# A three-stage transformer block on one core: last two products of the paired second layers swapped, two groups of additions made by accumulating transfers, places freed sooner, token products halved, and another order

## The chip, the core and the metric

The kernel runs on one core of a Trainium2 chip. The metric is device time in microseconds. Three runs of the kernel before took 1363.52, 1364.46 and 1368.9 us; the median is 1364.46 us. TensorE (PE in the profile) multiplies 128x128 weights, loaded beforehand (PEld), with a moving operand; VectorE (DVE) and ScalarE (ACT) do elementwise work; GpSimd (POOL) adds a little and issues accumulating transfers; SyncE (SP) issues nearly all other transfers.

## The reference

Soft-capped attention, then two residual stages: an MLP behind a layer norm, and a token-and-channel mixer.

```python
batch, n_heads, seq, head_dim = (4, 12, 448, 64)          # d_model 768
scores = cap * np.tanh(scale * (q @ k.T) / cap)
attn = softmax(scores)                                     # max subtracted, 1e-9 in the sum
x = (attn @ v) in (batch, seq, 768)
xn = (x - mean) / sqrt(var + 1e-6) * g_ln
x = x + relu(xn @ w_ch1) @ w_ch2                           # 768 -> 3072 -> 768
u = x + (relu(x.T @ w_tok1) @ w_tok2).T                    # tokens: 448 -> 256 -> 448
out = u + relu(u @ u_w_ch1) @ u_w_ch2                      # 768 -> 1536 -> 768
```

## The kernel before

Activations lie transposed: `X[b]` holds, for one of four batches, six tiles of 128 channels by 448 tokens. Products run with a number split into a rounded high part and a remainder (`split`, `low`, line 176), in three passes (`PASSES`, line 620), so a product over 128 channels is three matmuls of 448 columns. A layer's hidden units are worked in groups of 512: six groups in the first MLP, three in the second stage's channel MLP.

The program has three parts. (1) Attention of batches 0 and 1, then their layer norm. (2) Groups of the MLPs of batches 0 and 1 (`mlp`, `second_layer`), between which the heads of batches 2 and 3 and the token mixing of 0 and 1 (`tokens`) are laid. (3) Batches 2 and 3. Here most groups run as *pairs* (`strassen`, line 869): with seven block products in place of eight, each block product over sums of weight blocks and of the two batches. There are five such pair groups, then token mixing of 2 and 3, then two more. A pair group is one *block* in this text: `first_quads` (line 718) makes its hidden values H1, H2, H3, H4, H11, H21, H22, and `second_quads` (line 784) multiplies them by the second layer's tiles a11, a12, s1, s2, s3, s4, a22, three products of six matmuls for each tile pair.

The tiles a11, a12 and a22 come from DRAM as they are (`direct`). The tiles s1 to s4 are weight sums. `sums` (line 666) makes them by a chain on two working tiles: a plain transfer in (`start`), accumulating transfers issued by POOL (`more`, line 676), a negation on ACT (line 682), a split by ACT or DVE (lines 180, 182, 176) into the tile that PE reads. The working tiles are called `v`, `late_pair`, `late_vs` and `late_qk` in the profile; `late_vs` and `late_qk` serve the second half of a block's columns. The tiles that PE reads are eight half tiles taken in a ring (`part_ring`, line 664): a sum can only be split into a half tile whose last reader is done.

What a second-layer product is worth is added to X on DVE: `plus` (line 701) adds a bank of results, `both` (line 640) adds a finished tile: the lines 849 to 851 add w, the sum of s1 and s2 products, to X[3][r] and X[3][3+r], and line 858 adds t to X[2][3+r]. A block thus has nine such additions to X of one operand that is not a bank. Then come the products by s4 (`plus` into X[3][r]) and by a22 (`plus` into X[2][3+r]).

The order on each engine is made while the program is built. `Program.add` takes each step with the engines it may use, its cost in columns and a due time (`prog.key`); `emit` then hands out steps engine by engine, the earliest due among those that are ready by the planner's own costs (`FIXED`, `RATE`, `LATER`, lines 94 to 97). Engines work through their lists in that order. The numbers in lines 60 to 71 are due times and leads.

Storage is reused: `relay` (line 245) gives places of part 2 new names for part 3. `fill_weights` (line 274) waits for the readers of all old tiles in one list (line 291), `two`, which layer norm 3 uses, among them.

Of the kernel before, what the change touches and what calls it, by code (L numbers as in the profile page):

```python
# [59 lines left out]
URGENT, SCORES, PREPARE, LOAD = 1000.0, 19.31, 4.58, 24.58  # L60
# [4 lines left out]
T_LN0, T_LN1 = 7.69, -20.0  # L65
T_AHEAD, N_AHEAD, AHEAD_PACE = 14.0, 1, 5.0
T_ALONE, STRETCH0, T_PAIR, STRETCH1 = 85.0, 1.3, 165.0, 1.14
T_ATT2, PACE2, T_ATT3, PACE3 = 230.0, 35.0, 650.0, 25.0
LEAD, RAW_AHEAD, EVACUATE, TOKENS_AHEAD = 6.3, 9.57, -7.49, 17.25
N_WARM = 9  # L70
QUAD_LEAD, SUM_LEAD, SIDES_LATER, SIDES_PACE, X_LATER = 16.0, 24.0, 20.0, 4.0, 4.0
# [17 lines left out]
class Program:  # L89
# [5 lines left out]
    RATE = {"place": 0.0, "pe": 202.6e-3 / S, "act": 0.833e-3, "dve": 1.042e-3, "pool": 2.4e-3, "dma": 2.4e-3}  # L95
    LATER = {"pe": 0.16, "act": 0.1, "dve": 0.085, "pool": 0.05, "dma": 3.6}
# [59 lines left out]
def block_kernel(ctx: ExitStack, tc: tile.TileContext, qkv, cap, gln, w1, w2, wt1, wt2, con, out):  # L156
# [88 lines left out]
    def relay():  # L245
# [28 lines left out]
        def fill_weights():  # L274
# [6 lines left out]
            EXTRA[0].at, EXTRA[1].at = t[:, :, :CC], t[:, :, CC:]  # L281
            TWO.at = place("late_two", [2, S], F32R, tag="two")
# [8 lines left out]
        later([*WHOLE, PAIR, *V, *two, *QK, *KS, *VS], [*WF, *EXTRA, TWO, *TMP[:2]], fill_weights)  # L291
# [346 lines left out]

    def both(to, a, b, op, cols, early=0.0):
        add("dve+", cols, lambda: dve.tensor_tensor(to.at, a.at, b.at, op=op), [a, b], [to], early=early)  # L640
# [25 lines left out]
    def sums(chunks, a11, a12, a21, a22, s1, s2, s3, s4):  # L666
# [33 lines left out]
    def plus(to, bank, t):  # L700
        add("dve", S, lambda: dve.tensor_tensor(to.at, bank.at[:, :S], t.at, op=ALU.add), [bank, t], [to])  # L701
# [82 lines left out]
    def second_quads(g, last):  # L784
# [3 lines left out]
        tiles = dict(zip(("a11", "a12", "s1", "s2", "s3", "s4", "a22"), pairs))  # L788
# [50 lines left out]
        further(QUAD_LEAD)  # L839
# [4 lines left out]
        prog.key -= QUAD_LEAD  # L844
        direct("a22", 1, 2 * P)
        prog.key += QUAD_LEAD
        for r in range(3):
# [94 lines left out]
    def tokens(b, hidden):  # L942
# [55 lines left out]
        def second(half, hT):  # L998
            for e in range(3 * half, 3 * half + 3):
# [135 lines left out]
```

## Time and profile before

| | |
|---|---|
| median of three runs | 1364.46 us |
| the profiled execution | 1362.73 us, its span 1361.0 us |
| busy in the span | PE 1317.1, DVE 1160.7, ACT 766.7, POOL 236.6 us |
| parts in the span | heads and norm of batches 0, 1: to about 187; part 2: to about 790; first five blocks: about 838 to 1118; tokens of 2, 3: to 1224; last two blocks: to the end |

The busy time is the union of an engine's instructions. Matmuls overlap, so that what stands as idle before a matmul is somewhat less than what the next one starts late. The stretches of the profile tell where PE waits; the list of waits tells for whom.

### The profile page before, as it was taken

What the parts mean: (1) busy time and instruction counts of PE and PEld (TensorE: products, weight loads), DVE (VectorE), ACT (ScalarE), POOL (GpSimd) and SP (SyncE); (2) the same over time, 40 slices, a digit from 0 to 9 for tenths busy, and PEclk for the clock granted to TensorE, in tenths of its full rate; (3) what the DMA queues carried; (4) which work ended last, traced back from release to release, by engine and by line L of the source; (5) the groups of instructions that cost most, each with busy time, mean ns of one, the idle gap of its engine ahead of it and who ended that gap; (6) DMA issues with size and microseconds to landing.
All of it is one profiled execution on the core that took longest, in us unless ns stands there. A gap on an engine that the chain in (4) does not pass through costs nothing. (4 is left out here: it accounts for less than half of the span.)

```text
span 1361.0 us, 18258 instructions
## 1 busy us (share of the span) xinstructions
PE 1317.1 (97%) x6234; PEld 1128.5 (83%) x6234; DVE 1160.7 (85%) x1999; ACT 766.7 (56%) x1227; POOL 236.6 (17%) x196
## 2 busy tenths in 40 slices
PE   8899999999999999999999999899999999999997
PEld 4334589999999899988899989788988889999786
DVE  5989799999999999999999874878888884476698
ACT  8996667675766756866765322634535442223442
POOL 2420000110101001200000030333323320011221
PEclk9999999999999999999999999999999999999899
DMA  7885357777777868466777587687787884357685
GB/s 279 307 276 194 119 185 250 276 256 284 247 253 263 281 236 279 151 222 224 246 249 246 199 258 246 133 189 168 172 188 166 199 212 143 116 170 184 133 196 129
DMA packets 163021, 290.12 MB, mean 213 GB/s; under 512 B 12016, under 2 KB 105840, under 8 KB 162928
## 3 DMA queue, kind: packets, MB, share of 16 engines
q1 hardware_dynamic: 131888, 266.64, 57.9%
q0 software_dynamic: 30464, 22.03, 11.9%
q8 instruction: 49, 0.80, 0.3%
q10 hardware_dynamic: 576, 0.29, 0.1%
q14 instruction: 44, 0.36, 0.1%
HBM read 203.39 MB, written 85.52 MB: 212 GB/s over the span
## 5 line engine op out<-in xcount | busy, mean ns | idle before, releaser
L899 PE MATMUL bank<-h,split 128*128 128x448 f32 x1452 | 312.4, 368 | 4.0 <-DMA split<-kept 1.8
L926 PE MATMUL bank<-big,split 128*128 128x448 f32 x1404 | 299.2, 368 | 0.5 <-DVE split L176 0.5
L899 PEld LDWEIGHTS bank<-h,split 128*128 128x128 f32 x1452 | 271.4, 188 | 29.2 <-issue 3.6
L926 PEld LDWEIGHTS bank<-big,split 128*128 128x128 f32 x1404 | 262.6, 188 | 25.2 <-issue 1.6
L176 POOL TENSOR_TENSOR ks<-qk,ks 64x512 fp32r<-64x512 f32 x24 | 34.6, 1444 | 497.1 <-ACT ks L419 488.3
L903 DVE TENSOR_TENSOR x<-x,bank 128x448 f32<-128x448 f32 x121 | 73.8, 610 | 24.3 <-PE bank L899 23.6
L180 ACT ACTIVATE split<-whole 128x512 fp32r<-128x512 f32 (+1 forms) x70 | 50.4, 721 | 60.5 <-PE bank L899 24.5
L931 ACT ACTIVATE h<-bank 128x448 fp32r<-128x448 f32 x78 | 42.1, 540 | 64.5 <-PE bank L926 64.3
L333 ACT ACTIVATE whole<-raw 128x512 f32<-128x512 f32 (+2 forms) x94 | 70.7, 752 | 12.5 <-DMA raw<-in_w 6.8
L336 DVE SCALAR_TENSOR_TENSOR whole<-raw,whole 128x512 int32<-128x512 int32 (+2 forms) x94 | 74.1, 788 | 0.1
L337 DVE CUSTOM_DVE_ANT_0 whole<-raw,whole 128x1024 uint16<-128x1024 uint16 (+2 forms) x84 | 71.3, 849 | 0.1
L334 ACT ACTIVATE raw<-raw 128x512 int32<-128x512 uint32 (+2 forms) x94 | 71.2, 758 | 0.1
L176 DVE TENSOR_TENSOR split<-whole,split 128x512 fp32r<-128x512 f32 (+1 forms) x80 | 64.9, 812 | 0.8 <-ACT split L180 0.6
L446 DVE TRANSPOSE_TENSOR_REDUCE m<-x 128x28 f32<-128x896 f32 x48 | 52.9, 1105 | 12.3 <-ACT x L442 11.9
L441 ACT ACTIVATE own<-sc,tsc 128x896 f32<-128x896 f32 x48 | 48.2, 1004 | 15.2 <-DVE x L502 7.9
L713 PE MATMUL bank<-big,split 128*128 128x448 f32 x222 | 52.7, 375 | 2.3 <-ACT split L180 2.2
L932 DVE SCALAR_TENSOR_TENSOR h<-bank,h 128x448 fp32r<-128x448 f32 x78 | 47.7, 611 | 8.1 <-ACT h L931 7.9
L335 DVE TENSOR_SCALAR whole<-whole 128x512 int32<-128x512 int32 (+2 forms) x94 | 52.3, 557 | 1.9 <-ACT whole L333 1.8
L446 DVE TRANSPOSE_TENSOR_REDUCE m<-own 128x28 f32<-128x896 f32 x48 | 52.7, 1097 | 0.9 <-ACT own L442 0.9
L493 DVE TRANSPOSE_TENSOR_REDUCE n<-own 128x28 f32<-128x896 f32 x48 | 52.5, 1097 | 0.0
L442 ACT ACTIVATE own<-own,cap_t 128x896 f32<-128x896 f32 x48 | 50.0, 1042 | 0.6
L438 PE MATMUL sc<-qs,ks 128*128 128x448 f32 x192 | 48.1, 371 | 1.9 <-ACT own L441 1.4
(426 smaller groups left out, 2803.1 us busy)
## 6 DMA issues: line engine op xcount, KB each, us to landing
split<-kept SPq DMA_DIRECT2D x94, 384.0 KB, 4.4
raw<-in_w SPq DMA_DIRECT2D x36, 768.0 KB, 5.4
kept<-split SPq DMA_DIRECT2D x36, 768.0 KB, 4.2
raw<-in_w SPq DMA_DIRECT2D x54, 512.0 KB, 3.8
split<-kept SPq DMA_DIRECT2D x42, 512.0 KB, 3.9
keeps<-split SPq DMA_DIRECT2D x42, 512.0 KB, 3.8
qk<-in_qkv SPq DMA_DIRECT2D x33, 480.0 KB, 4.3
whole<-whole SPq DMA_DIRECT2D x28, 384.0 KB, 2.8
```

The source lines that it names most:

```text
L176: eng.tensor_tensor(out, whole, high.bitcast(F32), op=ALU.subtract)
L333: add("act", m * 1.1, lambda: act(f.bitcast(F32), hi.bitcast(F32), AF.Copy, scale=2.0 ** -112), [r], [w])
L334: add("act", m * 1.1, lambda: act(lo, lo.bitcast(U32), AF.Copy, scale=2.0 ** -29), (), [r])
L335: add("dve+", m // 2, lambda: dve.tensor_scalar(f, f, 3, None, op0=ALU.logical_shift_left), (), [w])
L336: add("dve+", m, lambda: dve.scalar_tensor_tensor(f, hi, -(1 << 31), f, op0=ALU.bitwise_and, op1=ALU.bitwise_or), [r], [w])
L337: add("pool+" if ahead else "dve+", m, lambda e: engine_of[e].tensor_tensor(f, f, lo, op=ALU.add), [r], [w])
L446: add("dve", 2 * S, lambda half=half, e=e: dve.tensor_reduce(m.at[:, half].rearrange("p c j -> p (c j)"), e.rearrange("p c (j i) -> p (c j ...
L493: add("dve", 2 * S, lambda half=half, e=e: dve.tensor_reduce(n.at[:, half].rearrange("p c j -> p (c j)"), e.rearrange("p c (j i) -> p (c j ...
L713: mm(bank.at[:, :S], w(wi), x.at[:, xi], start=(i, n) == (0, 0), stop=(i, n) == (len(parts) - 1, 2))
L899: mm(py.at[:, :S], w[:, wi, i * P:(i + 1) * P], h[i].at[:, hi], start=(i, n) == (0, 0), stop=(i, n) == (G - 1, 2))
L903: add("dve", S, lambda x=x, py=py: dve.tensor_tensor(x.at, x.at, py.at[:, :S], op=ALU.add), [py], [x], early=EVACUATE)
L926: mm(ph.at[:, :S], w[:, wi, cc * P:(cc + 1) * P], src[cc].at[:, xi], start=(cc, n) == (0, 0), stop=(cc, n) == (NCC - 1, 2))
```

## The change

1. `second_quads`: the products by a22 now stand ahead of those by s4; a22 gets the sixth pair of half tiles, s4 the seventh; the step of the chain that splits s4 is due later.
2. `onto`: of the nine additions, six (X[3][3+r] += w and X[2][3+r] += t) become accumulating transfers issued by POOL.
3. `relay`: `late_two` gets a filling of its own, so the rest no longer waits for `two`.
4. `second` in `tokens`: one step of six matmuls becomes two of three, the three of j=0 for each of three banks first.
5. Numbers: due times, leads, and the planner's costs, hence the order on all engines; `plus` has a lead of its own (`FIRST`).

```diff
-URGENT, SCORES, PREPARE, LOAD = 1000.0, 19.31, 4.58, 24.58
+URGENT, SCORES, PREPARE, LOAD = 1000.0, 12.03348, 11.42015, 28.4373
...
-        later([*WHOLE, PAIR, *V, *two, *QK, *KS, *VS], [*WF, *EXTRA, TWO, *TMP[:2]], fill_weights)
+        later([*WHOLE, PAIR, *V, *QK, *KS, *VS], [*WF, *EXTRA, *TMP[:2]], fill_weights)
+        later(two, [TWO], fill_two)
...
+    def onto(to, a):
+        add("pool", CC - 50, lambda: nc.gpsimd.dma_start(out=to.at, in_=a.at, accum_op=ALU.add), [a], [to], early=-X_LATER, lag=3.5)
...
-            add("pool", CC, lambda: nc.gpsimd.dma_start(out=shaped(f, at), in_=at, accum_op=ALU.add), boxes, [f], lag=4.0)
+            add("pool", CC - 50 if len(at.shape) == 2 else CC + 96, lambda: nc.gpsimd.dma_start(out=shaped(f, at), in_=at, accum_op=ALU.add), boxes, [f], lag=3.5)
...
-        tiles = dict(zip(("a11", "a12", "s1", "s2", "s3", "s4", "a22"), pairs))
+        tiles = dict(zip(("a11", "a12", "s1", "s2", "s3", "a22", "s4"), pairs))
...
             both(X[3][r], X[3][r], w[r], ALU.add, S, -X_LATER)
-            both(X[3][3 + r], X[3][3 + r], w[r], ALU.add, S, -X_LATER)
+            onto(X[3][3 + r], w[r])
...
-            both(X[2][3 + r], X[2][3 + r], t[r], ALU.add, S, -X_LATER)
+            onto(X[2][3 + r], t[r])
+            yield
+        for r in range(3):
+            plus(X[2][3 + r], times("a22", r, H4), X[2][3 + r])
+            final(2, 3 + r)
             yield
         for r in range(3):
             plus(X[3][r], times("s4", r, H22), X[3][r])
             final(3, r)
-            yield
-        for r in range(3):
-            plus(X[2][3 + r], times("a22", r, H4), X[2][3 + r])
-            final(2, 3 + r)
             yield
...
+            banks = {}
+            for j in range(2):
+                for e in range(3 * half, 3 * half + 3):
...
-                pe(6 * S, product, [*hT, *T2], [pu])
+                    pe(3 * S, product, [hT[j], T2[j]], [pu])
```

PE, the end of the third block, before. h_88 and h_89 are H3 (products by s3), h_82 and h_83 are H22 (by s4), eh and el are H4 (by a22).

```order
L713 MATMUL bank_111<-h_88,late_whole 128x448 x3
L713 MATMUL bank_111<-h_89,late_whole 128x448 x3
L713 MATMUL bank_112<-h_82,split_73 128x448 x3
L713 MATMUL bank_112<-h_83,split_73 128x448 x3
L713 MATMUL late_bank_5495<-h_82,split_73 128x448 x3
L713 MATMUL late_bank_5495<-h_83,split_73 128x448 x3
L713 MATMUL bank_113<-h_82,split_73 128x448 x3
L713 MATMUL bank_113<-h_83,split_73 128x448 x3
L713 MATMUL late_bank_5496<-eh_100,split_74 128x448 x3
L713 MATMUL late_bank_5496<-el_101,split_74 128x448 x3
```

The same place now:

```order
L719 MATMUL late_bank_5906<-h_88,late_whole 128x448 x3
L719 MATMUL late_bank_5906<-h_89,late_whole 128x448 x3
L719 MATMUL bank_112<-eh_100,split_73 128x448 x3
L719 MATMUL bank_112<-el_101,split_73 128x448 x3
L719 MATMUL late_bank_5907<-eh_100,split_73 128x448 x3
L719 MATMUL late_bank_5907<-el_101,split_73 128x448 x3
L719 MATMUL bank_113<-eh_100,split_73 128x448 x3
L719 MATMUL bank_113<-el_101,split_73 128x448 x3
L719 MATMUL late_bank_5908<-h_82,split_74 128x448 x3
L719 MATMUL late_bank_5908<-h_83,split_74 128x448 x3
```

The eighteen matmuls by a22 stand between s3 and s4.

PE, the first products of part 3, before. A run of nine on `big_80` or `big_81` is a direct product; `late_x`, `late_raw`, `late_own` are the activation sums.

```order
L713 MATMUL late_bank_5495<-late_raw,split_75 128x448 x9
L713 MATMUL bank_112<-late_x_6267,split_74 128x448 x9
L713 MATMUL bank_113<-late_own,split_75 128x448 x6
L713 MATMUL bank_113<-qs_97,split_75 128x448 x3
L713 MATMUL late_bank_5493<-big_80,split_73 128x448 x9
L713 MATMUL bank_111<-big_80,split_73 128x448 x9
```

Now:

```order
L719 MATMUL late_bank_5907<-late_raw,split_75 128x448 x9
L719 MATMUL late_bank_5905<-big_80,split_73 128x448 x9
L719 MATMUL bank_111<-big_80,split_73 128x448 x9
L719 MATMUL bank_112<-late_x_6231,split_74 128x448 x9
L719 MATMUL bank_113<-late_own,split_75 128x448 x6
L719 MATMUL bank_113<-qs_97,split_75 128x448 x3
```

The two direct products of the half tiles `split_73` stand two products (eighteen matmuls) sooner.

DVE, the end of the third block, now. `sq`, `sum`, `other` are w; `rstd`, `late_ks`, `late_qk` are t; L707 is `plus`, L646 is `both`.

```order
L646 TENSOR_TENSOR sq_94<-sq_94,rstd_110 128x448
L707 TENSOR_TENSOR late_ks<-late_bank_5908,late_ks 128x448
L707 TENSOR_TENSOR rstd_110<-late_bank_5905,rstd_110 128x448
L646 TENSOR_TENSOR sum_95<-sum_95,late_ks 128x448
L707 TENSOR_TENSOR late_qk<-bank_114,late_qk 128x448
L646 TENSOR_TENSOR x_79<-x_79,sq_94 128x448
L176 TENSOR_TENSOR split_74<-late_vs,split_74 128x384
L646 TENSOR_TENSOR other_96<-other_96,late_qk 128x448
L707 TENSOR_TENSOR late_ks<-bank_111,late_ks 128x448
L707 TENSOR_TENSOR late_qk<-late_bank_5906,late_qk 128x448
L646 TENSOR_TENSOR x_79<-x_79,sum_95 128x448
L707 TENSOR_TENSOR x_79<-late_bank_5905,x_79 128x448
```

The last row adds s3's first bank to X[3][3]; it now has to wait for the transfer that adds `sq`, which can go out after the first row; ten instructions stand between. Behind it, three rows on, stand the splits of `late_pair` and `v` for the next block. For the six transfers there stand 10, 9, 11, 14, 11 and 12 instructions between.

POOL at the same place, now; L643 is `onto`, L682 is `more`. Before, the L643 rows are not there.

```order
L682 DMA late_pair<-whole_16_180 128x384
L682 DMA late_qk<-whole_17_182 128x384
L643 DMA x_79<-sq_94 128x448
L643 DMA x_79<-sum_95 128x448
L682 DMA v<-whole_18_184 128x384
L643 DMA x_78<-rstd_110 128x448
L643 DMA x_79<-other_96 128x448
L643 DMA x_78<-late_ks 128x448
L643 DMA x_78<-late_qk 128x448
L682 DMA late_vs<-whole_19_186 128x384
```

Six additions stand among the accumulations of the next block's sums.

## Rows read from the trace of the kernel before

**Rows 1.** The page: busy time, share, instructions of each engine

```profile
PE 1317.1 (97%) x6234; PEld 1128.5 (83%) x6234; DVE 1160.7 (85%) x1999; ACT 766.7 (56%) x1227; POOL 236.6 (17%) x196
```

**Rows 2.** Stretches of the span: busy us (instructions), PE clock, DMA share, GB/s

```profile
0.00:102.00 102.00, 91.16 (x299) 38.40 (x300) 80.89 (x126) 92.73 (x119) 32.09 (x25) 0.98 0.82 288
102.00:187.00 85.00, 81.47 (x329) 50.85 (x328) 70.80 (x131) 51.37 (x71) 3.04 (x2) 1.00 0.48 157
187.00:790.00 603.00, 599.55 (x2974) 548.36 (x2973) 581.10 (x966) 396.11 (x602) 62.77 (x44) 1.00 0.70 243
790.00:904.00 114.00, 106.00 (x501) 94.47 (x501) 80.40 (x139) 40.66 (x80) 30.60 (x28) 0.99 0.78 213
904.00:1118.00 214.00, 208.02 (x1006) 187.19 (x1005) 186.95 (x357) 103.75 (x200) 67.71 (x62) 1.00 0.84 185
1118.00:1224.00 106.00, 105.28 (x547) 97.38 (x547) 55.84 (x93) 28.02 (x55) 9.47 (x8) 1.00 0.46 144
1224.00:1361.00 137.00, 125.65 (x587) 111.85 (x585) 104.72 (x194) 54.03 (x104) 30.89 (x27) 0.96 0.67 160
```

**Rows 3.** Timeline of PE at the second layers: start, us, [idle before <-releaser]

```profile
892.37 0.67 PE L713 MATMUL late_bank<-eh,split 128*128 128x448 f32 x2 [1.17 <-DMA split<-keeps]
...
947.53 0.47 PE L713 MATMUL late_bank<-h,split 128*128 128x448 f32 x1 [1.90 <-ACT split L180]
...
1001.16 1.26 PE L713 MATMUL bank<-h,split 128*128 128x448 f32 x3 [1.35 <-ACT split L180]
...
1054.78 1.27 PE L713 MATMUL late_bank<-h,split 128*128 128x448 f32 x3 [0.91 <-ACT split L180]
...
1347.22 1.27 PE L713 MATMUL bank<-h,split 128*128 128x448 f32 x3 [1.04 <-ACT split L180]
```

**Rows 4.** Timeline of ACT: the split of s4's second half, fourth block

```profile
1054.21 0.52 ACT L180 ACTIVATE split<-late_vs 128x384 fp32r<-128x384 f32 x1 [5.60 <-DMA late_vs<-wholes]
```

**Rows 5.** First block: timeline of PE and of ACT

```profile
849.87 2.02 PE L713 MATMUL bank<-big,split 128*128 128x448 f32 x9
...
867.13 2.98 PE L713 MATMUL bank<-big,split 128*128 128x448 f32 x9 [2.22 <-ACT split L180]
...
851.93 0.53 ACT L180 ACTIVATE split<-late_vs 128x384 fp32r<-128x384 f32 x1 [1.31 <-PE bank L713]
```

**Rows 6.** Stretches of 5 us, columns as in rows 2

```profile
865.00:870.00 5.00, 2.74 (x10) 2.26 (x11) 5.00 (x10) 3.82 (x8) 1.28 (x1) 0.89 0.31 63
870.00:875.00 5.00, 5.00 (x21) 4.55 (x20) 3.48 (x7) 3.41 (x8) 1.37 (x2) 0.77 0.57 71
1265.00:1270.00 5.00, 3.26 (x11) 2.62 (x11) 4.30 (x9) 2.69 (x6) 1.28 (x1) 0.83 0.61 131
1280.00:1285.00 5.00, 4.21 (x14) 3.80 (x15) 3.33 (x7) 2.32 (x5) 3.21 (x4) 0.69 0.44 77
```

**Rows 7.** The end: timeline, DVE (first and last of nineteen) and PE's last

```profile
1347.68 0.62 DVE L640 TENSOR_TENSOR x<-x,late_ks 128x448 f32<-128x448 f32 x1
...
1357.28 0.61 DVE L701 TENSOR_TENSOR x<-late_bank,x 128x448 f32<-128x448 f32 x1
...
1353.80 0.77 PE L713 MATMUL late_bank<-el,split 128*128 128x448 f32 x3
```

**Rows 8.** Line 676: duration ns min/median/max, first and last start; landing

```profile
L676 POOL DMA_DIRECT2D v<-whole x21: 859/862/1794, 797.9 to 1301.7; - x21
...
DMA to landing us min/median/max: 3.5/4.7/7.7
```

**Rows 9.** The page: POOL's DMA queue: packets, MB, share of 16 engines

```profile
q0 software_dynamic: 30464, 22.03, 11.9%
```

**Rows 10.** Waits of PE in 1260 to 1285: us in total, times, longest

```profile
PE bank L713 <- DVE late_whole L176: 1.6, 1, 1.6
PE late_bank L713 <- DVE split L182: 1.2, 1, 1.2
```

**Rows 11.** Waits of PE in 170 to 790

```profile
PE bank L1006 <- DVE h L993: 0.9, 2, 0.5
```

More of the change, by code (lines that the diff above doesn't have):

```diff
@@ L94 @@
     FIXED = {"place": 0.0, "pe": 0.0, "act": 0.067, "dve": 0.07, "pool": 0.15, "dma": 0.1}
-    RATE = {"place": 0.0, "pe": 202.6e-3 / S, "act": 0.833e-3, "dve": 1.042e-3, "pool": 2.4e-3, "dma": 2.4e-3}
-    LATER = {"pe": 0.16, "act": 0.1, "dve": 0.085, "pool": 0.05, "dma": 3.6}
+    RATE = {"place": 0.0, "pe": 202.6e-3 / S, "act": 0.833e-3, "dve": 0.001057, "pool": 2.4e-3, "dma": 2.4e-3}
+    LATER = {"pe": 0.16, "act": 0.147286, "dve": 0.047049, "pool": 0.05, "dma": 3.379172}
     ACROSS, ALONG = 0.09, 0.035
@@ L281, in fill_weights, with fill_two @@
             EXTRA[0].at, EXTRA[1].at = t[:, :, :CC], t[:, :, CC:]
+        def fill_two():
             TWO.at = place("late_two", [2, S], F32R, tag="two")
@@ L700, in plus @@
     def plus(to, bank, t):
-        add("dve", S, lambda: dve.tensor_tensor(to.at, bank.at[:, :S], t.at, op=ALU.add), [bank, t], [to])
+        add("dve", S, lambda: dve.tensor_tensor(to.at, bank.at[:, :S], t.at, op=ALU.add), [bank, t], [to], early=FIRST)
     def out_copy(to, bank):
@@ L838, in second_quads @@
             yield
-        further(QUAD_LEAD)
+        prog.key -= QUAD_LEAD
+        direct("a22", 1, 2 * P)
+        prog.key += QUAD_LEAD
         w = [next(tmps) for _ in range(3)]
@@ L843, in second_quads @@
             yield
-        prog.key -= QUAD_LEAD
-        direct("a22", 1, 2 * P)
-        prog.key += QUAD_LEAD
+        further(QUAD_LEAD)
         for r in range(3):
@@ L998, in second, with product @@
         def second(half, hT):
-            for e in range(3 * half, 3 * half + 3):
-                pu, xb, g = next(main_banks), X[b][e], u[e]
-                def product(e=e, pu=pu):
-                    a = (e % 3) * P
-                    for j in range(2):
+            banks = {}
+            for j in range(2):
+                for e in range(3 * half, 3 * half + 3):
+                    if j == 0:
+                        banks[e] = next(main_banks)
+                    pu, xb, g = banks[e], X[b][e], u[e]
+                    def product(e=e, pu=pu, j=j):
+                        a = (e % 3) * P
                         for n, (hi, wi) in enumerate(PASSES):
@@ L1007, in product @@
                                start=(j, n) == (0, 0), stop=(j, n) == (1, 2))
-                pe(6 * S, product, [*hT, *T2], [pu])
-                add("dve", S, lambda xb=xb, pu=pu: dve.tensor_tensor(xb.at, xb.at, pu.at[:, :S], op=ALU.add), [pu], [xb])
-                add("act", S, lambda xb=xb, g=g: act(g.at[:, 0], xb.at, AF.Copy), [xb], [g])
-                add("dve+", S, lambda xb=xb, g=g: low(dve, g.at[:, 1], xb.at, g.at[:, 0]), [xb], [g])
-                yield
+                    pe(3 * S, product, [hT[j], T2[j]], [pu])
+                    if j == 1:
+                        add("dve", S, lambda xb=xb, pu=pu: dve.tensor_tensor(xb.at, xb.at, pu.at[:, :S], op=ALU.add), [pu], [xb])
+                        add("act", S, lambda xb=xb, g=g: act(g.at[:, 0], xb.at, AF.Copy), [xb], [g])
+                        add("dve+", S, lambda xb=xb, g=g: low(dve, g.at[:, 1], xb.at, g.at[:, 0]), [xb], [g])
+                    yield
         hT = yield from first((yield from transposed(0)), False)
```

12 lines of the change are left out of this document (6 added, 6 removed).

## The prediction

> **What bounds the kernel now.** I read the page's busy line first, then the stretches, then PE's waits, and last the timeline around the waits that the change touches. PE is busy for 1317.1 of 1361.0 us [rows 1], and the change adds or removes no matmul. So all that can be won is the time in which PE stands still or runs slowly: 44 us in all. The stretches say where [rows 2]. The first 102 us hold 10.8 us of idle PE, but ACT is busy for 92.7 of them with the heads, so little of it is to be had. From 187 to 790 PE stands for 3.5 us only (603 less 599.55), while DVE is busy 96%. From 790 to 904, the run into the pair groups, it stands for 8.0; in the next four blocks (904 to 1118, 53.5 us each) for 6.0; in the tokens 0.7; from 1224 on for 11.4, of which 6.4 lie behind the last matmul, which ends at 1354.6 [rows 7].
>
> In the blocks the wait that ends last is nearly always one for a weight sum. The second-layer waits [rows 3] are 1.90, 1.35, 0.91 and 1.04 us for the split that makes s4, in the second, third, fourth and last block, and 1.17 for the transfer of a22 in the first. In the fourth block the split itself starts at once when its accumulating transfer lands [rows 4]: the chain of transfers, negations and splits was late, not ACT. The slow clock comes on top: behind a wait of 2.22 us in the first block [rows 5] the granted clock falls to means of 0.89 and 0.77 [rows 6], the lower level of 1.2 GHz for part of the time.
>
> **The change, part by part.** The sum is made against the profiled execution, 1362.73 us (span 1361.0); it is 1.7 us below the median of the three runs, 1364.46, and I add that at the end.
>
> *a22 before s4.* It removes nothing; it moves eighteen matmuls between s3 and s4. A matmul takes 208.02/1006 = 0.207 us in these blocks [rows 2], so s4 is wanted 3.7 us later than now. The waits for s4 [rows 3] are all shorter, so four of them, 5.2 us, go, and 1.8 us or more is left for transfers that come later than now. a22 is wanted 3.7 us sooner; its half tiles now come free with the last product by a12, not by s1, and three products by s1 (another 3.7 us), s2 and s3 stand between, so its wait of 1.17 may go as well. Bounds 0 and 6.4; I take 5.5. What is late next is s2, whose chain is one hop shorter and whose products stay where they were.
>
> *Order at the first block.* The wait of 2.22 us is for a sum in `late_vs`. Its chain begins with the split at 851.93, and that waited for PE [rows 5]: the product at 849.87, which reads the half tile that the split overwrites, had just ended. This product now stands eighteen matmuls sooner, so the chain can start some 3.7 us sooner, more than the 2.22. With the wait goes the slow clock behind it: (1 - 0.89) x 5 + (1 - 0.77) x 5 = 1.7 us [rows 6]. Bounds 0 and 3.9; I take 3, since every link behind the split is shared with other sums. The same kind of wait in the sixth block (1.2 and 1.6 us [rows 10], with the clock at 0.83 and 0.69 [rows 6]) stays: there the order of PE is the same as before but for a22 and s4.
>
> *Six additions by transfer.* In each of seven blocks DVE loses six additions. Nineteen instructions run back to back from 1347.68 to 1357.28 [rows 7], 0.533 us each, so 42 of them are 22.4 us of DVE. In the middle of part 3 that is hidden: DVE has 27 us of idle time in the four blocks already [rows 2]. At the end it shows: PE's last product is done at 1354.6, DVE's last instruction at 1357.9, and six of the nineteen go, 3.2 us. One of the waits counted above is part of this, so I take 2; bounds 0 and 3.2.
>
> The price is on POOL, in the transfers, and in a new wait. POOL pays 0.86 us for an accumulating transfer [rows 8], 5.2 us a block, and is busy for 67.7 of 214 [rows 2]: covered, unless one of the six stands in front of a sum and waits for DVE. The landing takes 3.5 to 7.7 us from the issue, 4.7 at the median [rows 8]. On DVE, ten instructions stand between the sum w and the addition that needs the transfer, 5.3 us; the least is nine, 4.8 us. So at the median nothing waits, and at the worst DVE waits 7.7 - 4.8 = 2.9 us a block, 20 in all. Queued behind that wait are the splits of `late_pair` and `v` for the next block, for which PE waits. No row shows such an addition, so both ends stay in the range. I take 0.35 us a block, 2.5, near the median row.
>
> The Trainium skill ("DMA: Bandwidth & Descriptors", "Anatomy of one DMA — SWDGE (gpsimd) path") gives a transfer issued by GpSimd a fixed 2.0 us and its bytes at 436 GB/s; an estimate for 224 KB is then 2.5 us, and DVE would never wait, which makes the sum 2.5 us better. Rows 8 have 4.7 for 192 KB in this kernel, and the trace decides.
>
> *Places freed sooner.* The sums of the first block need no longer wait for `two`. But the chain of rows 5 waited for PE's product, not for a place. Worth 0 (0 to 1).
>
> *Token products halved.* PE waited twice, 0.9 us in all, for the second half of the hidden units before the token product [rows 11]; the three matmuls of j=0 now need the first half alone, and two more banks are in use meanwhile. I take 0.5 (0 to 0.9).
>
> *Due times.* Heads of batches 2 and 3 come later: on PE the norm of batch 3 stands some 135 matmuls further back, the paired groups' first product 12. Up to 790 that takes work off DVE where it is busiest, but PE stands there for 3.5 us only [rows 2]. In front of the first block DVE had 33.6 us of idle time (790 to 904 [rows 2]), enough for what moves there. I take 1 there and 1 for the start, bounds -3 and 5.
>
> Sum: 5.5 + 3 + 2 + 0.5 + 2 - 2.5 = 10.5 us less. Profiled: 1352.2; as a median about 1354. I say 1353.5.
>
> **The rivals.**
>
> (a) *The transfers eat it.* POOL's queue takes 11.9% of 16 engines' span for 22.03 MB [rows 9], that is 112 transfers of 192 KB at 1.45 us of all sixteen. Six more a block, of 224 KB, are 8.7 to 10.1 us in 53.5, and the share rises from 0.84 [rows 2] to 1.0 or more, higher than in any long stretch here. If each landing in the chain (eight a block on `late_vs`) takes 0.4 us longer, s4 is 3 us later and the waits return, now in front of s4 again or of s2. For it: the share. Against it: 1.8 us or more of the 3.7 that s4 gets are room, and DVE's splits between the links come sooner with six instructions less in their way. Gain left: the first block, the tail, and little more: 1358 to 1365, no change.
>
> The skill's same page ("Issuing engines are not separate DMA queues") says that transfers of all issuing engines run on the same sixteen DMA engines and interleave. By that rule POOL's additions delay SP's loads as well; that sixteen engines are shared is what the share of rows 2 counts, and whether it delays here no row shows.
>
> (b) *DVE stops for the landing.* One mechanism: DVE works in order, and in each block the addition of s3's first bank stands in front of the next block's splits. If the landing is near the upper end of rows 8, DVE stands 2.9 us a block, and again up to 1.8 us (7.7 less eleven instructions) for X[2]. It costs PE when it goes beyond DVE's idle time of 27/4 = 6.7 us a block and beyond the time by which the first sums are ready ahead. From about 2 us a block on PE (7 x 2 = 14 against gains of 13) it makes the kernel slower; at 3 to 4: 1364.5 - 13 + 21 to 28 = 1372 to 1379. For it: bursts of six behind each other on POOL. Against it: the median.
>
> (c) *More than the sum.* The waits that I left alone (1.6 and 1.2 us in the sixth block, with 2.4 us of slow clock [rows 6, 10]) go too, since DVE's splits come sooner, the start gives 4, and nothing is paid: 1364.5 - 13 - 5.2 - 3 = 1343.
>
> (d) *No effect of the swap.* s4's chain moves with s4's due time (its split is now due later), so that it is as late as before. Then the first block, the tail and the due times are left, 7 less the price of 2.5: 1360, no change. Rows 4 speak against it: the split waited for a landing, not for its turn.
>
> **How the numbers follow.** Forecast (1346 to 1357.6) 0.48; (c) 0.12; (a) and (d) together 0.25; (b) 0.15. The range should leave out half of (b) and a part of (c): 1341 to 1368. What a measurement of this kernel can tell from no change is about 0.5%, 6.8 us: faster is below 1357.6, slower above 1371.3. Faster: forecast and (c), 0.60. Same: (a), (d) and the milder cases of (b), 0.28. Slower: 0.12.
>
> **What would show it.** Right: in PE's waits behind the second layers no wait for a split before s4's products; no wait of 2 us and no fall of the clock in the first block; DVE's last row of instructions ending within a microsecond or two of PE's last product; DVE's busy time some 22 us lower; landings of the new transfers near 5 us. Wrong: waits of DVE for transfers at line 707 with medians above 2 us; a DMA share above 0.95 in the blocks with periods of 53.5 us or more; new waits of PE for s2; the clock falling at a place where it did not before, above all where the norm of batch 3 now stands closer to the first block.

## The result and the profile after

The changed kernel takes 1378.89 us in the median of four runs (1377.34 to 1380.13), the kernel before 1365.62 beside it: a ratio of 1.0094, 95% interval 1.007 to 1.0119. It is slower by a little under one per cent, which is clear of the noise, and outside the forecast range of 1341 to 1368. The profiled execution took 1380.13 us, its span is 1378.0.

The page first: busy time by engine, then POOL's DMA queue with packets, MB and share of sixteen engines [rows 1, 9].

```profile
PE 1324.6 (96%) x6234; PEld 1135.4 (82%) x6234; DVE 1141.4 (83%) x1956; ACT 765.3 (56%) x1226; POOL 273.8 (20%) x240
...
q0 software_dynamic: 36512, 31.66, 15.6%
```

DVE has 19.3 us less to do (22.4 forecast), and POOL's queue carries 9.63 MB more, which is 42 transfers of 0.23 MB. PE is busy for 7.5 us more with the same matmuls, so it also ran slower. The stretches, with the columns of rows 2 (busy us of PE, PEld, DVE, ACT, POOL, then PE's granted clock, DMA share, GB/s), say where the time went:

```profile
187.00:790.00 603.00, 602.26 (x2994) 553.46 (x2993) 574.72 (x945) 391.66 (x591) 60.73 (x46) 1.00 0.72 245
790.00:904.00 114.00, 107.36 (x497) 94.72 (x497) 88.93 (x162) 46.34 (x90) 40.23 (x37) 0.96 0.85 218
904.00:1118.00 214.00, 198.70 (x933) 177.34 (x932) 165.34 (x309) 97.77 (x194) 79.89 (x78) 0.98 0.86 185
1118.00:1224.00 106.00, 99.89 (x515) 92.11 (x514) 48.75 (x84) 24.91 (x50) 9.73 (x11) 0.98 0.57 164
1224.00:1378.00 154.00, 141.63 (x673) 127.53 (x672) 114.03 (x204) 59.37 (x114) 49.93 (x45) 0.96 0.75 177
```

From 187 to 790 the change gains: PE stands for 0.7 us where it stood for 3.5 [rows 2]. In the blocks it stands for 15.3 of 214 us [rows 2: 6.0], and does 933 matmuls there where before it did 1006. In three of the last four stretches the clock is 0.02 or 0.03 lower than in rows 2. PE's waits from 835 us on (total, times, longest) begin with one that was small before: waits for line 701, which is line 707 now, came to 1.3 us in all there, and they come to 19.6 here.

```profile
PE late_bank L719 <- DVE x L707: 9.5, 6, 2.9
PE bank L719 <- DVE x L707: 6.1, 6, 2.4
PE bank L719 <- ACT split L180: 4.2, 2, 3.4
PE bank L966 <- DVE x L707: 4.0, 1, 4.0
```

Line 707 is `plus`, here the addition of a bank to X. The list of line 643, `onto`, says who waited for its transfers (us, times) and how long they took to land:

```profile
DVE x L707: 31.3, 34
...
DMA to landing us min/median/max: 3.2/9.2/13.2
```

DVE stood for 31.3 us, 34 times, for transfers that landed after 9.2 us at the median. The forecast took 4.7 from rows 8. While DVE waits it does not empty the bank, so PE stands; behind that the clock is lower:

```profile
890.30 0.62 DVE L707 TENSOR_TENSOR x<-late_bank,x 128x448 f32<-128x448 f32 x1 [0.67 <-DMA x<-sq]
890.98 2.33 PE L719 MATMUL late_bank<-h,split 128*128 128x448 f32 x6 [2.87 <-DVE x L707]
```

```profile
885.00:890.00 5.00, 3.11 (x16) 2.48 (x14) 1.14 (x3) 1.28 (x3) 2.34 (x3) 1.00 1.05 234
890.00:895.00 5.00, 2.98 (x8) 2.18 (x9) 3.41 (x6) 0.18 (x1) 1.73 (x2) 0.63 1.13 242
895.00:900.00 5.00, 4.97 (x18) 4.01 (x17) 3.20 (x6) 0.99 (x3) 0.00 (x0) 0.68 1.14 243
```

The timeline (start, us, what ended the idle time) shows DVE's addition released at 890.3 and PE 0.68 us later. The stretches of 5 us show the clock at 0.63 and 0.68 behind it, that is, the lower of its two levels, 1.2 GHz, for part of the time. This reads like rival (b). It was my first theory, and it fell: look at the DMA share in the same rows, 1.05 to 1.14.

### The profile page after: what moved, and what is told of

Read it like the earlier page. It is cut to its first block, busy times and chain, and to the rows that moved or that the text cites. A ratio compares the mean times of both kernels' runs of the same rounds, so it can differ in the third digit from the quotient of the medians.

```text
span 1378.0 us, 18205 instructions
## 1 busy us (share of the span) xinstructions
PE 1324.6 (96%) x6234; PEld 1135.4 (82%) x6234; DVE 1141.4 (83%) x1956; ACT 765.3 (56%) x1226; POOL 273.8 (20%) x240
## 3 DMA queue, kind: packets, MB, share of 16 engines
q0 software_dynamic: 36512, 31.66, 15.6%
## 5 line engine op out<-in xcount | busy, mean ns | idle before, releaser
L932 PEld LDWEIGHTS bank<-big,split 128*128 128x128 f32 x1404 | 262.8, 188 | 23.5 <-issue 1.9
L180 ACT ACTIVATE split<-whole 128x512 fp32r<-128x512 f32 (+1 forms) x64 | 45.7, 715 | 40.7 <-PE bank L905 18.3
L176 DVE TENSOR_TENSOR split<-whole,split 128x512 fp32r<-128x512 f32 (+1 forms) x80 | 67.7, 846 | 0.3 <-ACT split L180 0.2
L340 DVE CUSTOM_DVE_ANT_0 whole<-raw,whole 128x1024 uint16<-128x1024 uint16 (+2 forms) x84 | 67.0, 798 | 0.4
L449 DVE TRANSPOSE_TENSOR_REDUCE m<-x 128x28 f32<-128x896 f32 x48 | 52.8, 1104 | 11.5 <-ACT x L445 11.1
L719 PE MATMUL late_bank<-big,split 128*128 128x448 f32 x201 | 48.2, 379 | 6.0 <-DVE x L707 5.6
L449 DVE TRANSPOSE_TENSOR_REDUCE m<-own 128x28 f32<-128x896 f32 x48 | 52.8, 1099 | 0.9 <-ACT own L445 0.7
L719 PEld LDWEIGHTS bank<-big,split 128*128 128x128 f32 x222 | 44.0, 200 | 10.2 <-DVE x L707 6.4
```

Of the source, the lines that this page charges most:

```text
L176: eng.tensor_tensor(out, whole, high.bitcast(F32), op=ALU.subtract)
L340: add("pool+" if ahead else "dve+", m, lambda e: engine_of[e].tensor_tensor(f, f, lo, op=ALU.add), [r], [w])
L449: add("dve", 2 * S, lambda half=half, e=e: dve.tensor_reduce(m.at[:, half].rearrange("p c j -> p (c j)"), e.rearrange("p c (j i) -> p (c j ...
L719: mm(bank.at[:, :S], w(wi), x.at[:, xi], start=(i, n) == (0, 0), stop=(i, n) == (len(parts) - 1, 2))
L932: mm(ph.at[:, :S], w[:, wi, cc * P:(cc + 1) * P], src[cc].at[:, xi], start=(cc, n) == (0, 0), stop=(cc, n) == (NCC - 1, 2))
```

## The experiments

Each run was timed beside the kernel before on the same chip; its medians there were 1363.9 to 1366.7 us.

**Parts one at a time.** Four kernels: the changed one with the six additions as DVE instructions again (`onto(X, w)` back to `both(X, X, w, ALU.add, S, -X_LATER)`); before with the swap alone; before with `onto` alone; before with the numbers alone (item 5 of the change).

```diff
-            onto(X[3][3 + r], w[r])
+            both(X[3][3 + r], X[3][3 + r], w[r], ALU.add, S, -X_LATER)
...
-            onto(X[2][3 + r], t[r])
+            both(X[2][3 + r], X[2][3 + r], t[r], ALU.add, S, -X_LATER)
```

> The changed kernel with one part undone: the six additions of each block are DVE instructions again; the swap of the last two products, the due times, the places and the token halves stay. Theory (the landing): in the changed kernel DVE stands for the six transfers, PE waits 19.6 us at line 719 and in the tokens for banks and X that line 707 holds up, and nine stretches at half clock of 1.7 us each follow, against five before. Both should go: 1351 to 1361 us, block periods back near 54 us, no wait of DVE for a DMA at line 707. Rival (the new due times make the blocks late, the transfers only fall into the gap): 1372 or more, with the waits moved to the weight splits. Rival (the swap does it): also 1372 or more, with waits at the products by a22.

> The kernel before with the swap of the last two products alone, the old due times kept. Theory (the swap is good, as forecast, and the loss is elsewhere): the waits for the split of s4 go, 3 to 6 us less than before: 1359 to 1363. Rival (no effect, the split of s4 is due later and comes later): 1363 to 1368, waits for s4 as long as before. Rival (the swap is the loss): 1370 or more.

> The kernel before with the six additions of each block by accumulating transfers and nothing else. Theory (the landing): DVE stands at line 707 for them, median landing 8 us or more, periods of blocks 58 us and up: 1378 to 1395. Rival (due times or swap cause the loss): 1362 to 1368, as before, landings of the six near 5 us.

> The kernel before with the table of due times, the costs of the planner and the early addition behind a product alone; no swap, no transfers for the six additions, tokens whole. Theory (the landing): the new table is worth little, 1360 to 1367. Rival (the table makes the blocks late): 1374 to 1382, with periods of 58 us in the third to the fifth block although DVE waits for no transfer at the addition.

Measured: additions on DVE 1342.88 (ratio 0.9838, 0.9813 to 0.9863), swap alone 1369.43 (1.0039, 1.0021 to 1.0057), transfers alone 1379.88 (1.011, 1.0087 to 1.0133), numbers alone 1354.84 (0.9928, 0.9905 to 0.9951). So the six transfers lose 36 us beside the rest of the change and 16 alone; the rest is a good change. With the additions on DVE the clock is 1.00 in every stretch but the last (0.98), and the first entries of PE's waits from 830 us on are 2.4 and 1.9 us:

```profile
PE late_bank L719 <- DVE x L707: 2.4, 3, 1.7
PE bank L719 <- DVE x L707: 1.9, 2, 1.6
```

The page of this kernel, beside that of the changed one, says what the loss consists of:

```profile
PE 1308.4 (98%) x6234; PEld 1126.3 (84%) x6234; DVE 1160.5 (87%) x2002; ACT 764.3 (57%) x1222; POOL 236.6 (18%) x198
```

Between its span of 1338.6 us and the changed kernel's 1378.0 lie 39.4 us. In 23.2 of them PE stands, and 16.2 are the same 6234 matmuls taking longer (1324.6 for 1308.4), at a mean clock of 0.986 for 0.998.

Three of the four expectations missed. The theory's number was too high with the additions on DVE (1351 to 1361). The swap alone is slower, not faster. The numbers alone are worth more than expected (1360 to 1367).

**Is it DVE's wait?** Two kernels take the wait away and leave the transfers. In one they come behind the addition that needed them (X takes its product first; the last block adds on DVE). In the other DVE adds, and six accumulating transfers beside it go to a scratch area that nobody reads. A third only tells the planner of the late landing.

```diff
             plus(X[3][3 + r], p, X[3][3 + r])
+            if not last:
+                onto(X[3][3 + r], w[r])
```

```diff
             both(X[3][3 + r], X[3][3 + r], w[r], ALU.add, S, -X_LATER)
+            onto(next(spares), w[r])
```

```diff
-[a], [to], early=-X_LATER, lag=3.5)
+[a], [to], early=-X_LATER, lag=9.0)
```

> The changed kernel with the six transfers issued behind the addition that needed them, instead of ahead of it: X takes its product first and the transfer is added last, so that no instruction of the block waits for the landing; the last block, where X is stored at once, adds on DVE. Bytes, queue and POOL's work are those of the changed kernel in the other six blocks. Theory (DVE's wait): 1340 to 1350. Rival (the load on POOL's queue delays the sums and the splits): 1362 or more, PE's waits mostly for splits of weight sums, sums landing at 7 us and more.

> The changed kernel with the six additions of each block on DVE again, and beside them six accumulating transfers of the same tiles, of the same 224 KB and at the same place in POOL's order, to a scratch area in DRAM that nobody reads (filled with ones at the start, 24 small loads). It measures the load on POOL and the queue without DVE's wait; an accumulation into DRAM need not take what one into SBUF does. Theory (DVE's wait is nearly all of the 36 us between 1378.9 and 1342.9): 1343 to 1353. Rival (the sums of the weights stand behind the six in POOL's queue, and PE waits for their splits): 1363 to 1380, landings of the sums at 7 us and more.

> The changed kernel with one number changed: the planner takes 9.0 us instead of 3.5 for each of the six transfers to land (the median that the changed kernel's trace shows is 9.2), so that it puts other work of DVE ahead of the additions that need them. Theory (DVE stands in front of these additions, and what is queued behind it is what PE lacks): DVE's waits at line 707 for transfers fall from 31 us to under 12, and 1350 to 1362 us. Rival (the PSUM bank is held until the landing whatever DVE does meanwhile, or the transfers delay the sums in POOL's queue): the wait moves from DVE to the bank, 1370 or more.

Measured: transfers behind 1375.11 (1.0058, 1.0035 to 1.0081), transfers nobody needs 1382.04 (1.0103, 1.0082 to 1.0124), planned for 9 us 1401.41 (1.0257, 1.0235 to 1.028). The theory fell. With the transfers behind, DVE waits for none of them, and 32 of the 36 us are still lost. ACT does still wait, twice and 6.3 us in all, for a temporary that a transfer reads; a run below takes that away too. The third isn't a clean test: the planner put other things late too, and PE waited 43 us for tiles loaded by SP.

What is late instead is the first sum of the next block. Here is its chain with the transfers behind (timeline, fourth block's start): the accumulation into `v` is issued at 994.55, and the split that waits for it starts 8.7 us later; the next accumulation is issued at 1006.59 and its split comes at 1014.01; PE has stood for 4.2 us, the longest wait in the first row, which is from its list of waits.

```profile
PE late_bank L719 <- ACT late_whole L180: 5.2, 2, 4.2
```

```profile
994.55 1.48 POOL L682 DMA_DIRECT2D v<-whole  x1
1003.29 0.53 ACT L180 ACTIVATE late_whole<-v 128x384 fp32r<-128x384 f32 x1 [7.71 <-DMA v<-whole]
1006.59 1.57 POOL L682 DMA_DIRECT2D v<-whole  x1
1014.01 0.52 ACT L180 ACTIVATE late_whole<-v 128x384 fp32r<-128x384 f32 x1 [4.48 <-DMA v<-whole]
```

The same with the additions on DVE: 6.5 us from issue to split, and PE's wait at that place is 0.5 us.

```profile
984.31 0.86 POOL L682 DMA_DIRECT2D v<-whole  x1 [1.25 <-DMA v<-whole]
990.84 0.52 ACT L180 ACTIVATE late_whole<-v 128x384 fp32r<-128x384 f32 x1 [6.95 <-DMA v<-whole]
```

With transfers that nobody needs, DVE stands again and PE waits for a bank that DVE has not emptied, but what DVE waits for is ACT's split of that late sum:

```profile
954.20 0.53 ACT L180 ACTIVATE split<-v 128x384 fp32r<-128x384 f32 x1 [9.76 <-DMA v<-whole]
954.75 0.56 DVE L176 TENSOR_TENSOR split<-v,split 128x384 fp32r<-128x384 f32 x1 [4.17 <-ACT split L180]
957.44 2.12 PE L728 MATMUL bank<-big,split 128*128 128x448 f32 x9 [2.42 <-DVE x L716]
```

The same shows over all blocks. From 830 us on DVE waited for splits of weight sums by ACT for 20.8 us with the additions on DVE (11.4 and 9.4 in its list, for `late_whole` and `split`), for 47.4 with transfers that nobody needs and for 49.7 with the transfers behind. The landings of 7 us and more that the rival named did not quite come: into `v` they took 6.1 and 6.9 us at the median in these two runs, for 5.3 with the additions on DVE.

**Issues or bytes, POOL's queue or the engines?** Half the transfers (X[3] alone); scratch transfers of 56 columns instead of 448; the same load as plain copies by SP (twelve a block); and two loads that nothing waits for and that hold no temporary, from a constant tile, by POOL's queue (six accumulating) or by ACT's (twelve plain).

```diff
-nc.gpsimd.dma_start(out=to.at, in_=a.at, accum_op=ALU.add)
+nc.gpsimd.dma_start(out=to.at[:, :56], in_=a.at[:, :56], accum_op=ALU.add)
```

```diff
+        for _ in range(2):
+            add("dma", S, lambda to=to: nc.sync.dma_start(out=to.at, in_=a.at), [a], [to], early=-X_LATER)
```

```diff
-nc.gpsimd.dma_start(out=to.at, in_=a.at, accum_op=ALU.add)
+nc.gpsimd.dma_start(out=to.at, in_=t2.bitcast(F32)[:, 0, :S], accum_op=ALU.add)
```

```diff
+            add("act", 8, lambda to=to: nc.scalar.dma_start(out=to.at, in_=t2.bitcast(F32)[:, 0, :S]), [a], [to], early=-X_LATER)
```

> The changed kernel with three transfers a block instead of six: the additions to X[3] by transfer, those to X[2] on DVE. If each transfer costs its own share (the load on the queue, proportional): half of 36 us, 1357 to 1365. If the loss comes from the full burst alone (ten transfers of 1.6 us behind each other at the end of a block, against seven): 1343 to 1353. If DVE's wait were the cause, as I first thought (the runs with the transfers behind the additions, 1375, and with transfers that nobody needs, 1382, spoke against it): the three that remain have the shortest way to their addition, 1365 or more.

> As the run with six accumulating transfers to scratch that nobody needs (1382.0 us), but each moves 56 of the 448 columns: 28 KB instead of 224. POOL issues as many, of as many rows, and DVE, ACT and PE do the same work. Theory C (POOL's issuing time and the place in its order are what costs, 0.86 us and more each): 1370 to 1382. Theory A or B (the bytes, in the queue or the engines): 1343 to 1353.

> The kernel with the additions on DVE (1342.9 us), and for each of the six tiles two plain copies of 224 KB from the same tile to DRAM scratch, issued by SP, twelve a block: about as much work for the sixteen DMA engines as the six accumulating ones (plain transfers take about 0.74 us of all sixteen by the queue's share, two 1.5; an accumulating one 1.2), but not in POOL's queue. Theory A (what is lost is lost in POOL's queue, where the sums of the next block stand behind the six): 1343 to 1353. Theory B (the sixteen engines are full, whoever issues): 1365 to 1385, with the accumulating transfers of the sums landing later than 5 us and later than the 4.6 of the run with the additions on DVE. SP's own loads stand behind the copies in SP's queue in both cases.

> The kernel with the additions on DVE, and beside them six accumulating transfers of 224 KB a block in POOL's queue, from a constant tile (the weights of the token products) into DRAM scratch: nothing waits for them, they hold no temporary, only the queue and the engines carry them. Theory A or B (the bytes delay the next block's sums): 1362 to 1382, sums landing later than the 4.6 us of the run with the additions on DVE, PE's waits behind late splits. Rival (the temporaries held until the landing were the loss): 1343 to 1350.

> The kernel with the additions on DVE, and beside them twelve plain copies of 224 KB a block from a constant tile into DRAM scratch, issued by ACT in a queue of their own, with nothing waiting for them and nothing held. Theory A (POOL's queue is what is full): 1343 to 1352, plus what ACT pays for issuing. Theory B (the sixteen engines are full): 1362 to 1395, sums landing later, as with the copies on SP (1396.4).

Measured: three a block 1355.92 (0.994, 0.9917 to 0.9963), 13 of the 36 us and between the two ranges expected; small ones 1346.14 (0.9866, 0.984 to 0.9892); copies by SP 1396.35 (1.0228, 1.0198 to 1.0259), above both ranges; load on POOL's queue 1376.6 (1.0083, 1.006 to 1.0106); load by ACT 1373.91 (1.0067, 1.0041 to 1.0092).

It is bytes, not issues: POOL issues as many small ones, and 3 us are lost where the six of 224 KB to scratch lost 39. It isn't the temporaries either: the load on POOL's queue holds none, nothing waits for it, and 34 us are lost. And it isn't POOL's queue alone: with the load issued by ACT, that queue carries the same 30464 packets and 22.03 MB as before, and still the sums land late. Rows of DMA issues from 835 to 1100 us (times, KB, median us to landing), additions on DVE, then the load by ACT:

```profile
v<-whole POOLq DMA_DIRECT2D x14, 192.0 KB, 5.3
```

```profile
v<-whole POOLq DMA_DIRECT2D x14, 192.0 KB, 6.4
```

The other way round, loads by SP land later when the load is in POOL's queue (additions on DVE, then the load on POOL's queue):

```profile
split<-kept SPq DMA_DIRECT2D x30, 384.0 KB, 5.1
```

```profile
split<-kept SPq DMA_DIRECT2D x27, 384.0 KB, 7.0
```

The Trainium skill ("DMA: Bandwidth & Descriptors", "Issuing engines are not separate DMA queues") says that all issuing engines use the same sixteen engines and interleave; these two pairs of rows agree.

How the 36 us divide between POOL's queue and the shared engines stays open, since neither run that takes the load out of POOL's queue is pure. ACT makes the splits, and it spent up to 9.3 us issuing copies (ten of them at the end of the third block); its list of waits has 35.3 us in front of splits behind its own copies. With the copies by SP, transfers into `v` landed after 5.3 us, as with the additions on DVE, so that run lost its time otherwise, perhaps in SP's queue, where the sums' own first loads stand behind the copies.

How busy the engines are shows in three whole blocks, the second to the fourth. The table rests on one row of stretches for each kernel, from the start of the second block to that of the fifth, for instance (changed kernel, then additions on DVE):

```profile
894.40:1067.00 172.60, 161.81 (x757) 144.59 (x757) 130.50 (x245) 75.99 (x150) 66.06 (x64) 0.97 0.88 186
```

```profile
887.80:1046.20 158.40, 156.51 (x757) 141.80 (x758) 142.14 (x272) 76.83 (x149) 51.77 (x48) 1.00 0.83 178
```

A third of the row is the period, and period times share is what a block asks of the sixteen engines:

| kernel | period, us | DMA share | work of the sixteen, us a block |
|---|---|---|---|
| before | 53.9 | 0.81 | 43.7 |
| additions on DVE | 52.8 | 0.83 | 43.8 |
| the same, swap undone | 54.5 | 0.80 | 43.6 |
| small transfers | 53.1 | 0.86 | 45.7 |
| three a block | 55.0 | 0.85 | 46.8 |
| load by ACT | 58.3 | 0.85 | 49.6 |
| copies by SP | 59.8 | 0.84 | 50.2 |
| transfers behind | 57.3 | 0.88 | 50.4 |
| changed kernel | 57.5 | 0.88 | 50.6 |
| transfers nobody needs | 57.7 | 0.88 | 50.8 |
| load on POOL's queue | 58.0 | 0.88 | 51.0 |
| transfers alone | 57.6 | 0.89 | 51.3 |

Six transfers ask for 6.8 us more (50.6 less 43.8, 1.13 each), and every kernel that asks for about 50 needs 57 to 60 us a block, whichever queue carries it and whoever waits. The mean share does not sort them: at 0.86 the small transfers lose next to nothing, at 0.84 the copies by SP lose most. A mean of 0.88 looks like room, but the transfers come in a burst. At the end of the changed kernel's second block the share is above 1.0 for 25 us on end, and PE begins to stand in it and stands longest, 2.7 of 5 us, behind it:

```profile
931.00:936.00 5.00, 5.00 (x26) 4.38 (x25) 4.70 (x10) 1.96 (x5) 1.26 (x1) 1.00 1.05 247
936.00:941.00 5.00, 5.00 (x27) 4.63 (x26) 4.95 (x10) 1.88 (x4) 3.46 (x5) 1.00 1.06 225
941.00:946.00 5.00, 5.00 (x26) 4.64 (x25) 2.90 (x6) 0.00 (x0) 4.49 (x6) 1.00 1.08 237
946.00:951.00 5.00, 3.90 (x18) 2.94 (x17) 2.81 (x6) 1.47 (x3) 1.04 (x2) 1.00 1.13 227
951.00:956.00 5.00, 4.01 (x18) 3.23 (x18) 3.59 (x7) 0.13 (x1) 0.69 (x1) 1.00 1.13 255
956.00:961.00 5.00, 2.31 (x7) 1.83 (x8) 1.03 (x2) 1.98 (x4) 2.75 (x3) 0.86 0.76 163
```

With the additions on DVE none of these stretches, at the end of the same block, is above 1.0:

```profile
931.00:936.00 5.00, 5.00 (x27) 4.63 (x26) 5.00 (x10) 0.00 (x0) 0.00 (x0) 1.00 0.98 229
936.00:941.00 5.00, 5.00 (x26) 4.64 (x25) 4.87 (x11) 1.05 (x2) 1.75 (x2) 1.00 0.76 196
941.00:946.00 5.00, 4.51 (x21) 3.58 (x20) 3.08 (x7) 1.48 (x3) 1.28 (x1) 1.00 0.98 230
946.00:951.00 5.00, 4.75 (x23) 4.34 (x24) 4.00 (x9) 2.13 (x4) 1.77 (x2) 1.00 0.66 99
```

A share above 1.0 is not new by itself; the kernel before reaches 1.23 from 1080 to 1085. What is new is how long it lasts. Cut into such stretches from 835 to 1135 us, the share stays at 1.0 or more for at most 10 us on end before and with the additions on DVE, and for 15 with small transfers. It stays there for 20 or 25 us in every kernel with transfers of 224 KB in POOL's or ACT's queue, with three a block too. With the copies by SP it is 15, one more sign that they lose in another way.

**The tail.** Transfers in the last block alone, where no next sum can be late (`if last: onto(...)`, `else: both(...)`).

> The changed kernel with the six transfers in the last block alone, where no block follows whose sums could stand behind them; the other blocks add on DVE. Theory (forecast's term for the tail, 2 us, bounds 0 and 3.2, without the load on a next block): 1339 to 1342 against 1342.9 with all additions on DVE. Rival (the landings are late here too, DVE waits for them and ends later): 1343 to 1348.

Measured: 1347.15 (0.9871, 0.9842 to 0.9899). Up to the last block this program and the one with all additions on DVE have the same order on every engine, so the 4.3 us between their medians is not the edit's: from the start of the last block to the end of the span the one takes 59.4 us (1288.2 to 1347.6), the other 59.6. With no next block's sums under way the six transfers landed after 4.9 us at the median (3.2 to 6.8), close to the 4.7 of the forecast. What DVE saves it gives back in front of the last additions:

```profile
1339.47 1.82 DVE L707 TENSOR_TENSOR x<-late_bank,x 128x448 f32<-128x448 f32 x3 [1.65 <-DMA x<-sq]
...
1342.40 0.62 DVE L707 TENSOR_TENSOR x<-bank,x 128x448 f32<-128x448 f32 x1 [0.58 <-DMA x<-rstd]
```

**The swap.** The kernel with additions on DVE, its last two products back in the old order; later both side by side, since two nearly equal programs had differed by 4.3 us; and before with the swap and one number of the new table, `QUAD_LEAD` 3.1 for 16.

```diff
-        tiles = dict(zip(("a11", "a12", "s1", "s2", "s3", "a22", "s4"), pairs))
+        tiles = dict(zip(("a11", "a12", "s1", "s2", "s3", "s4", "a22"), pairs))
```

> As the run with the additions on DVE (1342.9 us), and the last two products also back in their old order (s4 before a22, a22's tiles loaded where they were); the new due times, places and token halves stay. Theory (the swap gains what was forecast, if the due times fit it): 1346 to 1350, with waits for the split of s4 again in front of its products. Rival (the swap has no effect): 1341 to 1345. Rival (the swap costs, as it did by 5.5 us under the old due times): 1334 to 1340.

> The changed kernel with its six additions on DVE, again, beside the next run on the same chip. If the swap gains what was forecast: 4 us or more below the next run, in the blocks (waits for the split of s4). If 6.8 us was the difference of two occasions: within 3 us of it.

> The same without the swap, beside the run before it on the same chip. If the swap gains what was forecast: 4 us or more above the run before it, with waits of PE for the split in front of s4's products. If 6.8 us was the difference of two occasions: within 3 us of it.

> The kernel before with the swap (1369.4 us) and one number of the new table, the lead of the loads of a11, a12, a22 and of the later sums' splits, 3.1 us instead of 16. If that lead is what the swap needs: 1357 to 1363. If it takes the rest of the table (heads, tokens, early additions): 1366 to 1373.

Measured: undone 1349.71 (0.988, 0.9861 to 0.99); side by side 1344.34 with the swap (0.9856, 0.9828 to 0.9883) and 1347.38 without (0.9887, 0.9863 to 0.9911); old table with the short lead 1369.7 (1.0033, 1.0015 to 1.0052). The side-by-side pair alone is unclear: 3.0 us, between the two expectations. Over all twelve runs of each the means differ by 5.7 us (3.4 to 8.2, by resampling the runs), but half of these runs were not side by side. The waits that the swap takes away under the new table are mostly those for a22's load; for s4's split there were one of 1.75 us in the sixth block and one of 0.5 in the last. Without the swap, third and fourth block:

```profile
994.97 0.67 PE L719 MATMUL late_bank<-eh,split 128*128 128x448 f32 x2 [0.94 <-DMA split<-keeps]
1048.02 0.67 PE L719 MATMUL bank<-eh,late_whole 128*128 128x448 f32 x2 [1.71 <-DMA late_whole<-keeps]
```

The lead alone isn't what the swap lacks under the old table. What is, stays open.

## Why the prediction was wrong, step by step

The gains came to about 22 us, where the sum had 13. The price came to 35, where it had 2.5, and the price decides. In the order of its steps, with the kernels that differ by one part each: before 1365, numbers 1354.8, and places and token halves 1349.0 (twelve runs), and swap 1343.4 (twelve runs), and transfers 1378.9. These are separate occasions, and two nearly equal programs differed by 4.3 us, so the smaller differences are rough.

- **a22 before s4, forecast -5.5: -5.7 over all runs beside the new numbers, -3.0 side by side.** The waits for s4's split went, as forecast, under the old numbers and in the changed kernel. But under the old numbers others came in front of s2 (1.45 and 1.13 us) and s3 (2.1), and the kernel was 5.5 us slower; under the new ones little of the gain was such a wait. So the reason is half right, and that the size came close is luck. Rows 3 were added up as if the planner would leave the rest in place.
- **First block, forecast -3, and due times and start, -2: together about -10.** The wait of 2.22 us is gone in the changed kernel and with the numbers alone, and still there with the swap alone: it was the order, as forecast. From the first block's first matmul to the second's it takes 56.3 us with the numbers alone, 62.2 before; twelve matmuls of other work fewer are in it.
- **Places and token halves, forecast -0.5: -5.9.** From the 2550th to the 3000th matmul of the trace, the stretch of token products, the kernel with the numbers alone takes 91.1 us and with these two 88.0; the waits of rows 11 were the smaller part. Which of the two edits gives the rest wasn't separated.
- **Six additions by transfer, forecast +2.5 and a tail of -2: +35.** This is the step that failed. The DVE time saved, 19 us for 22.4, was nearly right and worth nothing, since DVE was not what ended. The tail's 2 us are 0. The price was taken from the median landing of transfers in the kernel before [rows 8], as if six more of them would find the queues as those found them. In the burst they took 9.2 us at the median, and they delayed other transfers: the sums of the next block landed later, ACT's and DVE's splits came later, and PE stood. The forecast priced only DVE's wait for the six, and nothing for what they do to the next block's sums.
- **The rivals.** Rival (a) had the mechanism, the share of the sixteen engines. It took the load higher than it was (8.7 to 10.1 us a block for 6.8) and the price far lower, 5 to 12 us above the forecast, because s4 had room. The sums that were late were the next block's first, which have little: the room was looked for at the wrong products. Rival (b) had the time, 1372 to 1379, by the wrong mechanism: DVE does stop, for 31.3 us, yet only 3.8 us came back without it (1375.1 for 1378.9, intervals that overlap).
- **The signs.** Of those for a wrong forecast, new falls of the clock and periods above 53.5 us (57.5) came. Waits at line 707 came, but many and short, 31.3 us in 34, not "medians above 2 us". "Share above 0.95 in the blocks" came only in stretches of 5 us; in the stretch of 214 us it is 0.86, which hides it. New waits for s2 were not what cost the time.

The kernel with everything but the transfers takes 1343.4 us (ratios 0.9838 and 0.9856): it beats both.

## What to carry to other kernels

Moving work to the DMA engines from a compute engine that isn't the bound can cost more than it saves: here 19 us of DVE cost 35 us of the kernel. Read the DMA share in stretches of a few microseconds at the place where they would be issued, and ask whose transfer is next. A landing time measured at one load is no price at another. A wait that the profile names (DVE in front of its transfer) can be a companion of the loss and not its cause: take away the wait and keep the load before believing it.

## What the runs showed of the hardware

- An accumulating transfer of 224 KB between tiles cost about 1.13 us of all sixteen engines by period times share (six of them 6.8 us a block), and 1.26 by the shares of POOL's queue on the pages (15.6% of 1378.0 less 11.9% of 1361.0, for 42). It landed after 9.2 us at the median in the changed kernel, after 4.9 in the last block alone, after 3.2 at the least; the estimate of 2.5 in the prediction was reached by none.
- The share of the sixteen engines in a stretch of 5 us can stand above one (1.14 in the changed kernel, 1.23 once before). A mean of 0.88 over blocks went with a share above 1.0 for 25 us on end.
- Load in one queue delayed transfers in another: SP's loads of 384 KB landed after 7.0 us for 5.1 beside POOL's load, POOL's accumulations into `v` after 6.4 for 5.3 beside ACT's.
- Two programs with the same order on every engine up to the last 59 us differed by 4.3 us in medians of six runs each, on two chips, so a few microseconds between separate runs say little.
